# Two output stores a step in place of four, x rows loaded earlier, and a rearranged opening in a Fourier-and-mixer kernel

## The chip, the core and the metric

The kernel runs on one core of a Trainium2 chip. The core has a matrix engine (TensorE, in the rows PE, with its weight loads as PEld), a vector engine (VectorE, DVE), an engine for elementwise functions (ScalarE, ACT), a general engine (GpSimd, POOL) and one that here only issues transfers (SyncE, SP). Transfers between the chip's memory (DRAM) and the core's SBUF are carried by 16 DMA engines. Matrix products land in PSUM. The metric is the device time of one execution in microseconds (us).

## What is computed

Two stages over x of 8 batches, 3136 positions and 256 features. The first is the real part of a two-dimensional Fourier transform, the second a mixer: a rank-32 product along the positions, then a two-layer perceptron along the features, each added to its input.

```python
def _attn_ref(x):                       # x: 8, 3136, 256
    X = np.fft.fft(x, axis=1)
    X = np.fft.fft(X, axis=2)
    return X.real.astype(np.float32)

def _moe_ref(x, U, V, w_ch1, w_ch2):    # U: 3136x32, V: 32x3136, w_ch1: 256x1024, w_ch2: 1024x256
    xt = x.transpose(0, 2, 1)
    h = xt @ U @ V
    u = x + h.transpose(0, 2, 1)
    ch = np.maximum(u @ w_ch1, 0.0) @ w_ch2
    return (u + ch).astype(np.float32)
```

## The kernel before

Position n is split as n1*64 + n2 (49 by 64), an output position as k2*49 + k1. The kernel goes through the batches in four pairs. The symmetries of a real transform let lines k1 and 49-k1 be made together, so 25 values of k1 serve all 49.

**Front.** Tables, the transformed weights and the first batch (loaded and transformed by a path of its own, `load_single`, `te_single`) are made before the main loop. There each batch's rank-32 product ends in `te` (L282), is turned into `TT` by `te_turn` (L285) and multiplied into the hidden layer's basis by `te_hidden` (L299), which gives `TE`.

**Loading a pair.** Eight chunks. Of each, `load_pair_chunk` (L97) issues two transfers on SP: `xa` (L103) and, for the mirrored rows of the other half, `xb` (L107). Each is 98 rows of 4 KB. In DRAM, the 98 rows of `xa` are one run of equal strides, while `xb` reads its rows backwards and so has them as 2 batches of 49 rows:

```python
in_=bass.AP(x.tensor, x.offset + r * 4 * D, [[N1 * 64 * D, 2], [-64 * D, N1], [1, 4 * D]])
```

`fold_pair_chunk` (L145, POOL) adds `xa` and `xb` into `y`; `fold_pair_chunk_d` (L154) adds and subtracts the halves of the features into `yb`: two operations on DVE (L141, L142) and a copy of two columns on ACT (L143). `s1_steps` multiplies `yb` on PE into `z`, which is written to DRAM (`zturn`, L206), and `turn` (L273) reads it back the other way round into `g`. From `g` the `lines` steps make `q`, the transformed lines; each also sends one row of `q` to `VZ` with a small transfer (L383).

**The main loop.** A pair has 12 chunks of two steps and a short last one: 25 output tiles. In a step `mlp1` makes two groups of the hidden layer of the present chunk on PE (even and odd products from `q`, L425, then the rank-32 product from `TE` and `VZ`, L432), ACT copies one half (`ab`, L435), DVE makes the even and odd combinations with the maximum (L438, L441), and `mlp2` makes one output tile of the chunk before (L480, L490). Between the two phases of `mlp2` stands an empty ACT instruction (L492) by which PE's second phase waits for the first (the bank turn). `drain` copies the tile to `om` (ACT, L521), adds and subtracts into `ob` (POOL, L522, L523) and stores it with four transfers on SP (L527), each 64 rows of 1 KB.

**What sets the order.** The order is written out by hand (`manual_schedule`): `plan(p)` gives each of a pair's 26 steps a list of further work, and `place_next` spreads the loading of the next pair over them. For chunk c it starts at step a + gap*c with the load; 2 steps later comes the fold on POOL, 4 later the fold on DVE, 5 later the products. Each engine works through its list in order, SP too. SP's transfers use eight semaphores in turn, so a transfer's issue waits until the eighth transfer before it has landed. `ob` has four buffers.

Of the kernel before, what the change touches and what calls it, by code (L numbers as in the profile page):

```python
# [22 lines left out]
def kernel(  # L23
# [115 lines left out]
    def fold_d(yb, src, l0, l1):  # L139
        o, i = yb[:, l0:l1, :], src[:, l0:l1, :]  # L140
        nc.vector.tensor_tensor(o[:, :, 1:128], i[:, :, 1:128], i[:, :, 255:128:-1], op=AL.add)  # L141
        nc.vector.tensor_tensor(o[:, :, 129:256], i[:, :, 1:128], i[:, :, 255:128:-1], op=AL.subtract)  # L142
        nc.scalar.copy(o[:, :, 0:129:128], i[:, :, 0:129:128])  # L143

    def fold_pair_chunk(ck):  # L145

# [135 lines left out]
        nc.scalar.mul(te[0:rows, 0:129], ps[0:rows, 0, 0:129], 0.5)  # L282
        nc.scalar.mul(te[0:rows, 129:256], ps[rows:2 * rows, 0, 129:256], 0.5)

    def te_turn(pr, bs):  # L285
        ps = bank2("tt")
        n = 32 * len(bs)
        for blk in range(2):
            nc.tensor.matmul(ps[:, 0, 64 * blk:64 * blk + n], te[0:n, blk::2], eye[0:n, 0:n],
                             start=(blk == 0), stop=True, skip_group_check=True)  # L290
        for i, b in enumerate(bs):
            o = TT[pr.p % 2][b]
            src = ps[:, 0, 0:128].rearrange("p (k r) -> p k r", k=2)[:, :, 32 * i:32 * i + 32]
            copy_dve(o[:, :, 0:32], src)
            copy_act(o[:, :, 64:96], src)

    def te_hidden(pr, b, cs=None):
        o = TE[pr.p % 2][b]
# [56 lines left out]
    def lines(pr, b, c, evac, now=False):  # L355

        q = q_tile(pr)
        ps = [bank2("ln")] * 2
        if now:
            ps[1] = bank2("ln")  # L360
        for i in range(4):
            for blk in range(2):
                for s in range(2):
                    line(pr, b, ps[s][:, s, 256 * blk + 64 * i:256 * blk + 64 * i + 64], 8 * c + 1 + 2 * i + s, blk,
                         i == 0 and blk == 0)
        c0 = b * 1536 + 512 * c
        if now:
            return lambda evac: lines_out(q, ps, b, c, evac, now)
        lines_out(q, ps, b, c, evac, now)
# [41 lines left out]
    def mlp1_parts(ch, u):  # L411
        q, c0, w = ch.pr.q, ch.c0, ch.w
        m = 512 // w
        if u == 0:
            ch.h = hpool.tile([P, 2, JT, 256], BF16, tag="h", name="hT")
        ps = bank2("hps")
        for i in range(m):
            j = m * u + i
# [3 lines left out]
            for blk in range(2):  # L422
                for s in range(2):
                    lt = W1z[64:P, ja] if s and blk == 0 else W1p[c][64 * s:64 * s + 64, blk, jc]
                    nc.tensor.matmul(o[s], lt, q[64 * s:64 * s + 64, blk, c0:c0 + w], start=(i == 0 and blk == 0),  # L425
                                     stop=True, skip_group_check=True)
        yield
        for i in range(m):
            ja = slice((m * u + i) * P, (m * u + i + 1) * P)
            for b, a, n, v in ch.parts:  # L430
                for s in range(2):
                    nc.tensor.matmul(ps[:, s, i * w + a:i * w + a + n], TE[ch.p % 2][b][64 * s:64 * s + 33, ja],  # L432
                                     VZ[64 * s:64 * s + 33, b, v:v + n], start=False, stop=True, skip_group_check=True)
# [5 lines left out]
        if not ch.mini:  # L439
            flip = [v.rearrange("p i (t n) -> p (i t) n", n=P) for v in [h[:, 0], a, b]]  # L440
            nc.vector.tensor_tensor(flip[0][:, :, ::-1], flip[1], flip[2], op=AL.max)  # L441
            if u == 0:
                ch.qr = apool.tile([P, 2, 256], BF16, tag="qr", bufs=3, name="qr")
                copy_act(ch.qr.rearrange("p k (t n) -> p k t n", n=P)[:, :, :, ::-1],
                         q[:, :, c0:c0 + 256].rearrange("p k (t n) -> p k t n", n=P))
# [8 lines left out]
    def mlp2(ch, t, mixed):  # L454
# [56 lines left out]
        def drain(eng):  # L511
            n = 1 if ch.mini else 2
            po = st.ps[:, 0:n, 0:D].rearrange("p a (b d) -> p a b d", b=2)
            ob = opool.tile([P, 2, D], FP32, tag="ob", name="ob")
            om = opool.tile([P, 2, 2, P], FP32, tag="om", bufs=3, name="om")[:, 0:n]
            a = om[:, :, 0]
            if eng is nc.vector:
                nc.scalar.copy(om[:, :, 1], po[:, :, 1])
                a = po[:, :, 0]
            else:  # L520
                nc.scalar.copy(om, po)  # L521
            eng.tensor_tensor(ob[:, 0:n, 0:P], a, om[:, :, 1], op=AL.add)  # L522
            eng.tensor_tensor(ob[:, 0:n, P:D], a, om[:, :, 1], op=AL.subtract)  # L523
            for i in range(n):
                for hf, (b, k) in enumerate(ch.units[t]):
                    r = slice(64 - 64 * hf, 128 - 64 * hf) if i else slice(64 * hf, 64 * hf + 64)
                    nc.sync.dma_start(out=out[b].rearrange("(k2 k1) d -> k1 k2 d", k1=N1)[N1 - k if i else k], in_=ob[r, i])  # L527

        st.phase, st.drain = phase, drain
        if not mixed:  # L530
# [72 lines left out]
    nc.gpsimd.dma_start(out=uv[0:32], in_=moe_V)  # L603
    idle = W1z[:, 0:640]
    nc.vector.memset(idle.bitcast(FP32), 0.0)
    nc.sync.dma_start(out=VZ[96:97].rearrange("p b j -> p (b j)").rearrange("p (a j) -> p a j", j=640), in_=idle[0:5])

    wps = bank2("warm")[:, 0]

# [113 lines left out]
    for t in [x for y in TT for x in y]:  # L723
        nc.gpsimd.memset(t[:], 0.0)
        nc.gpsimd.memset(t[64:65, 0, 32:33], 1.0)
    nc.gpsimd.memset(V0[:].bitcast(FP32), 0.0)
    gate = tmp([64, 4], "gate")
    nc.gpsimd.tensor_copy(gate[0:1, 0:1], an2[0:1, 0, 0:1])
    bp_mask, bp_sin = residual_tables(nc.gpsimd)
# [58 lines left out]
    def v_copy(k0, k1, first=True):  # L788
# [3 lines left out]
            nc.sync.dma_start(out=VS[32:64, 0, cs], in_=VZ[64:96, 0, cs])  # L792
        elif first is None:
            v2 = [VS[:, i, cs].rearrange("p (w n) -> p w n", n=P) for i in range(2)]
            copy_dve(v2[1][0:32, :, ::-1], v2[0][0:32])
            ts(v2[1][32:64, :, ::-1], v2[0][32:64], -1.0, None)
        else:
            for r in (0, 64):
                nc.sync.dma_start(out=VZ[r:r + 32, 1, cs], in_=VZ[r:r + 32, 0, cs])
# [16 lines left out]
    nc.scalar.mul(W1p[0][:], w1ps[:], 0.5)  # L816
    nc.scalar.mul(W1z[64:P, 0:512], w1ps[64:P, 0], sgh[64:P])
    bp_sin()
    te_single(first, 0, teps)
    lps = lines(first, 0, 0, None, now=True)  # L820
    te_turn(first, [0])
    lps([copy_act, copy_dve])
    w1ps = bank2("w1ps")
    w1_fold(1, w1ps)
    te_hidden(first, 0, 0)
    nc.scalar.mul(W1p[1][:], w1ps[:], 0.5)
    nc.scalar.mul(W1z[64:P, 512:1024], w1ps[64:P, 0], sgh[64:P])
    w2_fold(0, nc.gpsimd)
# [12 lines left out]
    hpool = ctx.enter_context(tc.tile_pool(name="hpool", bufs=2))  # L841
    apool = ctx.enter_context(tc.tile_pool(name="apool", bufs=2))

    pairs = [first] + [Pair(p) for p in range(1, NP)]
    chunks = [ch for p in range(NP) for ch in pair_chunks(p)]
    NCK = len(chunks) // NP
    NS = 2 * NCK
    W1T = xpool.tile([P, 2, 2, 512], BF16, tag="xa", name="w1t")
# [9 lines left out]
    def product():  # L858
        ps = bank2("w12")
        for blk in range(2):  # L860
            for j in range(JT):
                nc.tensor.matmul(ps[:, blk, 0:D], W1T[:, j // 4, blk, (j % 4) * P:(j % 4 + 1) * P], W2[:, j, :],
                                 start=(j == 0), stop=(j == JT - 1))
        m = ps[:, :, 0:D]

        copy_act(G[:], m)
        nc.gpsimd.memset(RR[0][0:64].bitcast(FP32), 0.0)
        nc.gpsimd.memset(RR[1][0:64].bitcast(FP32), 0.0)
        for blk in range(2):
            ts(RR[0][64:P, blk], m[64:P, blk], sgm[64:P, blk:blk + 1], None)  # L870
        for blk in range(2):
            o = slice(blk * P, (blk + 1) * P)
            nc.vector.tensor_tensor(G[:, blk, o], G[:, blk, o], Bp[:, blk], op=AL.add)
            nc.vector.tensor_tensor(RR[0][64:P, blk, o], RR[0][64:P, blk, o], Bp[64:P, blk], op=AL.add)
            nc.vector.tensor_copy(RR[0][0:64, blk, o], Bp[0:64, blk])
            nc.vector.tensor_copy(RR[1][0:64, blk, o], Bp[0:64, blk])
            ts(RR[1][64:P, blk], RR[0][64:P, blk], sg[64:P, blk:blk + 1], None)

    def pair_tables():

# [31 lines left out]
    def plan(p):  # L912
# [11 lines left out]
        def place_next(nx, a, gap):  # L924

            s1 = list(s1_steps(nx, [copy_act, copy_dve]))
            for c, (load, fn, fd) in enumerate(load_steps(nx)):
                for o, f in [(0, load), (2, fn), (4, fd), (5, s1[2 * c]), (5, s1[2 * c + 1])]:
                    at[int(a + gap * c) + o].append(f)
            e = int(a + gap * 7) + 5  # L930
            at[e].append(lambda: (turn(nx, 0), turn(nx, 1)))
            at[e + 1].extend(te_steps(nx))
            at[e + 2].append(lambda: te_turn(nx, [0, 1]))
# [4 lines left out]
        if p == 0:  # L938
            rest = []
            at[0].append(lambda: te_hidden(cur, 0, 1))  # L940
            at[0].append(lambda: lines(cur, 0, 1, both))
            at[0].append(lambda: (w1_turn(0), w1_turn(1)))
            at[1].append(product)
            at[1].append(lambda: v_copy(1, 9, None))
            mid[2].append(lambda: te_direct(cur, 0))
            at[2].append(lambda: (v_lines(nc.gpsimd, 9, 17), v_copy(9, 17), lines(cur, 0, 2, both)))
            at[3].append(lambda: (v_lines(nc.gpsimd, 17, NK1), v_zero(nc.gpsimd), rest.append(pair_tables())))
            at[5].append(lambda: v_copy(9, 17, None))
            at[5].append(lambda: (v_copy(17, NK1), v_copy(0, 1), v_copy(0, NK1, False), rest[0]()))
            at[6].append(lambda: nc.sync.dma_start(out=T[64:P], in_=T[0:64]))  # L950
# [7 lines left out]
            at[13].append(lambda: lines(cur, 1, 1, both))  # L958
            at[15].append(lambda: lines(cur, 1, 2, both))
            at[18].append(lambda: (zero_line(cur, 0, copy_act), zero_line(cur, 1, copy_act)))  # L960
            place_next(pairs[1], 4, 1.75)
        else:
            at[0].append(lambda: lines(cur, 0, 1, both))
            at[2].append(lambda: te_hidden(cur, 1))
# [3 lines left out]
                at[7 + 3 * c].append(lambda c=c: lines(cur, 1, c, both))  # L968
            at[16].append(lambda: (zero_line(cur, 0, copy_act), zero_line(cur, 1, copy_act)))
            if p + 1 < NP:  # L970
                place_next(pairs[p + 1], 0, 2.3)
        return at

    for i in range(len(chunks) + 1):
# [7 lines left out]
        for t in range(2):  # L982
            m = None
            us_ = [] if cur is None else [t] if cur.mini else [2 * t, 2 * t + 1]
            n = 2 * (i % NCK) + t
            if len(us_) == 2:
                mlp1(cur, us_.pop(0))
            if prv is not None and t < len(prv.units):
# [43 lines left out]
```

## Time and profile before

| | |
|---|---|
| two runs | 613.29 and 614.98 us, median 614.13 |
| the profiled execution | 616.54 us; its span, first to last instruction, 614.3 us |
| mean granted TensorE clock | 0.875 |
| steps (one output tile each) | 100 |
| bytes moved by DMA | 65.53 MB, 107 GB/s over the span |
| out stores on SP | 392, of 64 KB each |

All times in the rows are of that one execution, and the sums of the prediction are made against its span, which is within 0.2 us of the runs' median. A wait row reads: engine, tile and line that waited, what it waited for, total us, number of waits, longest. A row of stretches gives the busy time of PE, PEld, DVE, ACT and POOL (with the number of instructions), the granted clock as a share of full speed, the mean busy share of the 16 DMA engines, and GB/s moved. With one DMA engine of 16 busy throughout, the share is 0.06. A timeline row gives start, duration, engine and line; the duration covers all instructions merged in it.

### The profile page before, as it was taken

How to read it: one execution, taken by the hardware profiler on the slowest of the kernel's cores; microseconds unless marked ns; L12 is line 12 of the kernel's file. 1: busy time of each engine (PE TensorE's matmuls, PEld its weight loads, DVE VectorE, ACT ScalarE, POOL GpSimd, SP SyncE). 2: the span in 40 equal slices, each digit the busy share in tenths (PEclk: the TensorE clock that was granted, in tenths of full speed). 3: DMA queues.
4: the chain of work that ended last, by engine and by line, in shares of the span. 5: the costliest groups of instructions: out<-in, count | busy, mean ns of one | idle time of the engine just before them, and what ended most of it. 6: DMA issues, size and time to landing. Idle time of an engine off the chain costs nothing. (4 is left out here: it accounts for less than half of the span.)

```text
span 614.3 us, 19104 instructions
## 1 busy us (share of the span) xinstructions
PE 485.0 (79%) x8159; PEld 384.2 (63%) x8159; DVE 356.6 (58%) x592; ACT 279.0 (45%) x505; POOL 249.4 (41%) x342
## 2 busy tenths in 40 slices
PE   4788798294869798886584979878677498999995
PEld 3658575183758476674462847756456285888894
DVE  7567894253764376564465337746456545676673
ACT  5665344152633455353342345534334235656552
POOL 7285334633451234444535124453453512333340
PEclk9788997686978798797795879988869589999998
DMA  8571334444338324334342832443434282233333
GB/s 158 172 106 25 88 110 108 133 117 137 102 109 180 82 91 121 124 100 128 96 126 64 174 88 90 118 130 95 128 93 126 63 180 67 56 75 71 73 80 79
DMA packets 60751, 65.53 MB, mean 107 GB/s; under 512 B 13593, under 2 KB 53496, under 8 KB 60504
## 3 DMA queue, kind: packets, MB, share of 16 engines
q1 hardware_dynamic: 56426, 59.45, 37.2%
q0 software_dynamic: 4160, 4.66, 4.3%
q8 instruction: 63, 1.03, 0.7%
q10 hardware_dynamic: 80, 0.20, 0.1%
q14 instruction: 22, 0.18, 0.1%
HBM read 34.62 MB, written 32.19 MB: 109 GB/s over the span
## 5 line engine op out<-in xcount | busy, mean ns | idle before, releaser
L480 PE MATMUL ops<-W,hT 64*128 64x256 bf16 x3072 | 224.7, 287 | 48.4 <-ACTq L492 41.3
L438 DVE SCALAR_TENSOR_TENSOR hT<-ab,hps 128x512 bf16<-128x512 bf16 x200 | 136.6, 683 | 172.3 <-ACT ab L435 172.2
L480 PEld LDWEIGHTS <-hT 64*128 64x128 bf16 x3072 | 158.9, 100 | 85.7 <-ACTq L492 44.6
L435 ACT CAST ab<-hps 128x512 bf16<-128x512 f32 x200 | 117.0, 590 | 127.1 <-PE hps L432 107.1
L425 PE MATMUL hps<-q,W1p 64*128 64x256 bf16 (+1 forms) x1248 | 131.3, 281 | 13.0 <-DVE hT L441 11.2
L151 POOL TENSOR_TENSOR y<-xa,xb 98x510 f32<-98x510 f32 (+1 forms) x48 | 58.1, 1231 | 192.6 <-DMA xb<-in_x_dram 184.1
L522 POOL TENSOR_TENSOR ob<-om 128x256 f32<-128x256 f32 (+1 forms) x97 | 78.0, 804 | 142.5 <-ACT om L521 121.3
L441 DVE TENSOR_TENSOR hT<-hps,ab 128x512 bf16<-128x512 f32 x192 | 130.8, 681 | 0.0
L425 PE MATMUL hps<-q,W1z 64*128 64x256 bf16 (+1 forms) x416 | 106.3, 282 | 0.0
L432 PE MATMUL hps<-VZ,TE 33*128 33x256 bf16 (+1 forms) x896 | 84.5, 273 | 27.4 <-DMA VZ<-q 27.1
L425 PEld LDWEIGHTS <-W1p 64*128 64x128 bf16 x1248 | 72.9, 99 | 31.0 <-DVE hT L441 19.4
L523 POOL TENSOR_TENSOR ob<-om 128x256 f32<-128x256 f32 (+1 forms) x97 | 78.2, 806 | 0.0
L141 DVE TENSOR_TENSOR yb<-y 98x508 bf16<-98x508 f32 (+1 forms) x24 | 33.8, 1409 | 62.7 <-POOL y L151 62.6
L432 PEld LDWEIGHTS <-TE 33*128 33x128 bf16 x896 | 44.4, 100 | 34.7 <-issue 28.4
L521 ACT COPY om<-ops 128x512 f32<-128x512 f32 (+1 forms) x97 | 56.4, 581 | 9.9 <-PE ops L490 9.8
L490 PE MATMUL ops<-TK,VS 64*128 64x256 f16 x192 | 54.6, 284 | 0.5 <-ACT TK L80 0.5
L425 PEld LDWEIGHTS <-W1z 64*128 64x128 bf16 x416 | 41.0, 99 | 3.0 <-issue 2.1
L490 PEld LDWEIGHTS <-qr 64*128 64x128 bf16 x384 | 38.2, 100 | 3.6 <-issue 0.4
L143 ACT CAST yb<-y 98x8 bf16<-98x8 f32 (+1 forms) x24 | 5.5, 227 | 76.9 <-POOL y L152 76.9
L490 PEld LDWEIGHTS <-q 64*128 64x128 bf16 x384 | 38.2, 100 | 2.8
L490 PE MATMUL ops<-R,qr 64*128 64x256 f16 x192 | 38.9, 284 | 0.0
L490 PE MATMUL ops<-R,q 64*128 64x256 f16 x192 | 38.8, 284 | 0.0
(181 smaller groups left out, 483.0 us busy)
## 6 DMA issues: line engine op xcount, KB each, us to landing
out_dram<-ob SPq DMA_DIRECT2D x392, 64.0 KB
xa<-in_x_dram SPq DMA_DIRECT2D x24, 392.0 KB
xb<-in_x_dram SPq DMA_DIRECT2D x24, 392.0 KB
zturn<-z SPq DMA_DIRECT2D x9, 512.0 KB
g<-zturn SPq DMA_DIRECT2D x6, 416.0 KB
g<-zturn SPq DMA_DIRECT2D x6, 384.0 KB
X<-in_x_dram POOLq DMA_DIRECT2D x4, 384.0 KB, 8.1
X<-in_x_dram POOLq DMA_DIRECT2D x2, 744.0 KB, 8.1
```

The source lines that it names most:

```text
L141: nc.vector.tensor_tensor(o[:, :, 1:128], i[:, :, 1:128], i[:, :, 255:128:-1], op=AL.add)
L151: nc.gpsimd.tensor_tensor(ck.y[:, l0:l1, 1:256], ck.xa[:, l0:l1, 1:256], rb[:, l0:l1, 255:0:-1], op=AL.add)
L425: nc.tensor.matmul(o[s], lt, q[64 * s:64 * s + 64, blk, c0:c0 + w], start=(i == 0 and blk == 0), stop=True, skip_group_check=True)
L432: nc.tensor.matmul(ps[:, s, i * w + a:i * w + a + n], TE[ch.p % 2][b][64 * s:64 * s + 33, ja], VZ[64 * s:64 * s + 33, b, v:v + n], start=F ...
L435: nc.scalar.copy(ab[:], ps[:, 1])
L438: nc.vector.scalar_tensor_tensor(h[:, 1], b, -1.0, a, op0=AL.mult, op1=AL.max)
L441: nc.vector.tensor_tensor(flip[0][:, :, ::-1], flip[1], flip[2], op=AL.max)
L480: mm = nc.tensor.matmul(op, ch.h[rows[half], s, j, t * P:(t + 1) * P], W2[rows[half], j, :], start=(ha == 0 and j == 0), stop=False, skip_ ...
L490: last = nc.tensor.matmul(*g[k], start=False, stop=(k == len(g) - 1), skip_group_check=True)
L521: nc.scalar.copy(om, po)
L522: eng.tensor_tensor(ob[:, 0:n, 0:P], a, om[:, :, 1], op=AL.add)
L523: eng.tensor_tensor(ob[:, 0:n, P:D], a, om[:, :, 1], op=AL.subtract)
```

## The change

- **Stores.** A full step's tile is stored with two transfers in place of four. Each now writes lines k and k+1 (or 49-k-1 and 49-k) together, from all 128 partitions. In DRAM the destination is 2 lines of 64 rows of 1 KB. The short last chunk keeps its 64-row stores.
- **Loads.** The folds and products of a chunk stand two steps later behind its load: the fold on POOL 4 steps after it, the one on DVE 6, the products 7. Chunks follow each other by 2 steps (2.3 before), in the first pair the first load comes at step 2 (4 before).
- **Fold copy.** L143's copy of two columns is on DVE, not on ACT.
- **Front.** The even and odd products of the first chunk (`mlp1_parts` up to its first `yield`) are issued ahead of `te_hidden`, the rank-32 part, and finished in step 0. The first `lines` uses one PSUM tile, and is drained before `te_turn`.
- **Tables.** `product` adds `Bp` on PE instead of DVE, and the rest of its rows are copied by ACT (`product_rows`). `VZ`'s zero row is set by POOL and not by a transfer. `v_lines` on POOL all stand in step 0; two table copies go from DVE to ACT. `qr` is copied after the second group of the hidden layer, not the first.

On SP, a stretch in the middle of the second pair's steps, before (`out_dram<-ob` are stores, `xa` and `xb` the loads, `VZ` the small rows, `zturn` the spill of `z`; the shape is the destination's):

```order
L103 DMA xa<-in_x_dram 98x1024
L107 DMA xb<-in_x_dram 98x1x1024
L527 DMA out_dram<-ob 64x256 x4
L383 DMA VZ<-q 1x16x32
L206 DMA zturn<-z 128x2048
L527 DMA out_dram<-ob 64x256 x8
```

and the same stretch of the changed kernel:

```order
L103 DMA xa<-in_x_dram 98x1024
L107 DMA xb<-in_x_dram 98x1x1024
L529 DMA out_dram<-ob 2x64x256 x2
L381 DMA VZ<-q 1x16x32
L529 DMA out_dram<-ob 2x64x256 x2
L103 DMA xa<-in_x_dram 98x1024
L107 DMA xb<-in_x_dram 98x1x1024
L529 DMA out_dram<-ob 2x64x256 x2
L206 DMA zturn<-z 128x2048
```

A step's four stores of 64x256 have become two of 2x64x256, the loads come every second step, and the spill of a chunk comes later behind the loads it came from.

On ACT, around one fold copy of the second pair, before:

```order
L521 COPY om<-ops 128x512
L435 CAST ab<-hps 128x512
L80 COPY qr<-q 128x4x128
L435 CAST ab<-hps 128x512
L143 CAST yb<-y 98x8
L521 COPY om<-ops 128x512
L435 CAST ab<-hps 128x512 x2
```

On DVE in the changed kernel, around the same copy:

```order
L436 SCALAR_TENSOR_TENSOR hT<-ab,hps 128x512
L439 TENSOR_TENSOR hT<-hps,ab 128x4x128
L141 TENSOR_TENSOR yb<-y 98x4x127
L142 TENSOR_TENSOR yb<-y 98x4x127
L143 CAST yb<-y 98x8
L436 SCALAR_TENSOR_TENSOR hT<-ab,hps 128x512
L439 TENSOR_TENSOR hT<-hps,ab 128x4x128
```

The copy stood on ACT between `ab` and `om`, with the bank turn behind it; it now follows the two fold operations on DVE.

The diff, cut to its core:

```diff
     def fold_d(yb, src, l0, l1):
...
-        nc.scalar.copy(o[:, :, 0:129:128], i[:, :, 0:129:128])
+        nc.vector.tensor_copy(o[:, :, 0:129:128], i[:, :, 0:129:128])
...
     def mlp1_parts(ch, u):
-        if u == 0:
-            ch.h = hpool.tile([P, 2, JT, 256], BF16, tag="h", name="hT")
         ps = bank2("hps")
...
         yield
+        if u == 0:
+            ch.h = hpool.tile([P, 2, JT, 256], BF16, tag="h", name="hT")
...
-            for i in range(n):
+            rows = out.rearrange("b (k2 k1) d -> b k1 k2 d", k1=N1)
+            if ch.mini:
                 for hf, (b, k) in enumerate(ch.units[t]):
-                    r = slice(64 - 64 * hf, 128 - 64 * hf) if i else slice(64 * hf, 64 * hf + 64)
-                    nc.sync.dma_start(out=out[b].rearrange("(k2 k1) d -> k1 k2 d", k1=N1)[N1 - k if i else k], in_=ob[r, i])
+                    nc.sync.dma_start(out=rows[b, k], in_=ob[64 * hf:64 * hf + 64, 0])
+            else:
+                b, k = ch.units[t][0]
+                for i, k in enumerate([k, N1 - k - 1]):
+                    nc.sync.dma_start(out=rows[b, k:k + 2], in_=ob[:, i])
...
     te_single(first, 0, teps)
-    lps = lines(first, 0, 0, None, now=True)
-    te_turn(first, [0])
-    lps([copy_act, copy_dve])
+    lines(first, 0, 0, None, now=True)([copy_act, copy_dve])
     w1ps = bank2("w1ps")
     w1_fold(1, w1ps)
+    te_turn(first, [0], copy_dve)
+    first.u = [mlp1_parts(ch0, i) for i in range(2)]
+    next(first.u[0])
     te_hidden(first, 0, 0)
+    next(first.u[1])
...
             for c, (load, fn, fd) in enumerate(load_steps(nx)):
-                for o, f in [(0, load), (2, fn), (4, fd), (5, s1[2 * c]), (5, s1[2 * c + 1])]:
+                for o, f in [(0, load), (4, fn), (6, fd), (7, s1[2 * c]), (7, s1[2 * c + 1])]:
                     at[int(a + gap * c) + o].append(f)
-            e = int(a + gap * 7) + 5
+            e = int(a + gap * 7) + 7
...
-            place_next(pairs[1], 4, 1.75)
+            place_next(pairs[1], 2, 1.75)
...
-                place_next(pairs[p + 1], 0, 2.3)
+                place_next(pairs[p + 1], 0, 2)
...
+            if i + t == 0:
+                for g in first.u:
+                    next(g)
+                us_ = []
```

More of the change, by code (lines that the diff above doesn't have):

```diff
@@ L283, in te_out, with te_turn @@
         nc.scalar.mul(te[0:rows, 129:256], ps[rows:2 * rows, 0, 129:256], 0.5)
-    def te_turn(pr, bs):
+    def te_turn(pr, bs, eng=copy_act):
         ps = bank2("tt")
@@ L294, in te_turn @@
             copy_dve(o[:, :, 0:32], src)
-            copy_act(o[:, :, 64:96], src)
+            eng(o[:, :, 64:96], src)
     def te_hidden(pr, b, cs=None):
@@ L358, in lines @@
         ps = [bank2("ln")] * 2
-        if now:
-            ps[1] = bank2("ln")
         for i in range(4):
@@ L441, in mlp1_parts @@
             nc.vector.tensor_tensor(flip[0][:, :, ::-1], flip[1], flip[2], op=AL.max)
-            if u == 0:
+            if u == 1:
                 ch.qr = apool.tile([P, 2, 256], BF16, tag="qr", bufs=3, name="qr")
@@ L605 @@
     nc.vector.memset(idle.bitcast(FP32), 0.0)
-    nc.sync.dma_start(out=VZ[96:97].rearrange("p b j -> p (b j)").rearrange("p (a j) -> p a j", j=640), in_=idle[0:5])
     wps = bank2("warm")[:, 0]
@@ L726 @@
     nc.gpsimd.memset(V0[:].bitcast(FP32), 0.0)
+    nc.gpsimd.memset(VZ[96:97].bitcast(FP32), 0.0)
     gate = tmp([64, 4], "gate")
@@ L794, in v_copy @@
             v2 = [VS[:, i, cs].rearrange("p (w n) -> p w n", n=P) for i in range(2)]
-            copy_dve(v2[1][0:32, :, ::-1], v2[0][0:32])
-            ts(v2[1][32:64, :, ::-1], v2[0][32:64], -1.0, None)
+            copy_act(v2[1][0:32, :, ::-1], v2[0][0:32])
+            nc.scalar.mul(v2[1][32:64, :, ::-1], v2[0][32:64], -1.0)
         else:
@@ L818 @@
     bp_sin()
+    pairs = [first] + [Pair(p) for p in range(1, NP)]
+    chunks = [ch for p in range(NP) for ch in pair_chunks(p)]
+    ch0 = chunks[0]
+    ch0.pr = first
     te_single(first, 0, teps)
-    lps = lines(first, 0, 0, None, now=True)
-    te_turn(first, [0])
-    lps([copy_act, copy_dve])
+    lines(first, 0, 0, None, now=True)([copy_act, copy_dve])
     w1ps = bank2("w1ps")
     w1_fold(1, w1ps)
+    te_turn(first, [0], copy_dve)
+    first.u = [mlp1_parts(ch0, i) for i in range(2)]
+    next(first.u[0])
     te_hidden(first, 0, 0)
+    next(first.u[1])
     nc.scalar.mul(W1p[1][:], w1ps[:], 0.5)
@@ L842 @@
     apool = ctx.enter_context(tc.tile_pool(name="apool", bufs=2))
-    pairs = [first] + [Pair(p) for p in range(1, NP)]
-    chunks = [ch for p in range(NP) for ch in pair_chunks(p)]
     NCK = len(chunks) // NP
@@ L862, in product, with product_rows @@
                 nc.tensor.matmul(ps[:, blk, 0:D], W1T[:, j // 4, blk, (j % 4) * P:(j % 4 + 1) * P], W2[:, j, :],
-                                 start=(j == 0), stop=(j == JT - 1))
+                                 start=(j == 0), stop=False, skip_group_check=True)
+        for blk in range(2):
+            nc.tensor.matmul(ps[:, blk, blk * P:(blk + 1) * P], eye[:], Bp[:, blk], start=False, stop=True, skip_group_check=True)
         m = ps[:, :, 0:D]
         copy_act(G[:], m)
-        nc.gpsimd.memset(RR[0][0:64].bitcast(FP32), 0.0)
-        nc.gpsimd.memset(RR[1][0:64].bitcast(FP32), 0.0)
+        copy_dve(RR[0][64:P], m[64:P])
         for blk in range(2):
[L870 to L877, printed above, removed]
+            ts(RR[1][64:P, blk], m[64:P, blk], sg[64:P, blk:blk + 1], None)
+        for r in RR:
+            nc.vector.tensor_copy(r[64:65, 0, 0:P], Bp[64:65, 0])
+            nc.vector.memset(r[64:65, 0, P:D].bitcast(FP32), 0.0)
+    def product_rows():
+        for r in RR:
+            nc.gpsimd.memset(r[0:64].bitcast(FP32), 0.0)
+            for blk in range(2):
+                nc.scalar.copy(r[0:64, blk, blk * P:(blk + 1) * P], Bp[0:64, blk])
     def pair_tables():
@@ L942, in plan @@
             at[0].append(lambda: (w1_turn(0), w1_turn(1)))
+            at[0].append(product_rows)
+            at[0].append(lambda: (v_copy(1, 9, None), v_lines(nc.gpsimd, 9, 17), v_lines(nc.gpsimd, 17, NK1), v_zero(nc.gpsimd)))
             at[1].append(product)
-            at[1].append(lambda: v_copy(1, 9, None))
             mid[2].append(lambda: te_direct(cur, 0))
-            at[2].append(lambda: (v_lines(nc.gpsimd, 9, 17), v_copy(9, 17), lines(cur, 0, 2, both)))
-            at[3].append(lambda: (v_lines(nc.gpsimd, 17, NK1), v_zero(nc.gpsimd), rest.append(pair_tables())))
+            at[2].append(lambda: (v_copy(9, 17), lines(cur, 0, 2, both)))
+            at[3].append(lambda: rest.append(pair_tables()))
             at[5].append(lambda: v_copy(9, 17, None))
```

## The prediction, made before the changed kernel ran

> **What bounds the kernel now.** I read the page's shares and slices first, then stretches by pair, then who waited for whom, then SP's queue.
>
> ```profile
> PE 485.0 (79%) x8159; PEld 384.2 (63%) x8159; DVE 356.6 (58%) x592; ACT 279.0 (45%) x505; POOL 249.4 (41%) x342
> ...
> 48.00:212.00 164.00, 125.57 (x2133) 99.63 (x2130) 91.64 (x160) 67.43 (x129) 67.42 (x88) 0.84 0.42 110
> 212.00:365.50 153.50, 120.06 (x1881) 91.37 (x1882) 85.37 (x120) 65.29 (x122) 61.30 (x74) 0.84 0.42 111
> 365.50:516.00 150.50, 116.87 (x1883) 89.97 (x1881) 84.98 (x120) 65.16 (x122) 61.32 (x74) 0.88 0.42 112
> 516.00:612.00 96.00, 89.57 (x1700) 79.81 (x1694) 62.46 (x101) 52.23 (x92) 31.82 (x46) 0.99 0.31 71
> ```
>
> The four stretches are the four pairs. The last one loads nothing: 25 steps in 96 us, 3.8 us a step, PE busy for 93% of it at clock 0.99. The other three take 150 to 164 us, with 34 to 38 us of them without PE work and the clock at 0.84 to 0.88. So PE bounds the last pair, and something in the loading of the next pair bounds the first three.
>
> ```profile
> POOL y L151 <- DMA xb<-in_x_dram: 184.1, 22, 15.0
> ACT yb L143 <- POOL y L152: 76.9, 18, 11.2
> DVE yb L141 <- POOL y L151: 62.6, 18, 9.7
> PE ops L480 <- ACTq L492: 41.3, 11, 8.7
> PE hps L432 <- DMA VZ<-q: 27.1, 5, 11.6
> ...
> SPq L527 <- POOL ob L523: 101.9, 46, 12.3
> SPq L527 <- DMA xb<-in_x_dram: 81.3, 18, 5.9
> ```
>
> It is one chain. POOL's fold waits for `xb`, ACT's copy L143 waits for the fold, the bank turn L492 stands behind that copy on ACT, and PE waits for the turn: 41.3 us. SP's stores wait 81.3 us for an `xb` eight transfers earlier, and a small row of `VZ` behind such a store costs PE another 27.1 us. At the root is one slow transfer. Why it is slow shows in stretches where nothing else moves:
>
> ```profile
> 225.60:230.30 4.70, 4.63 (x98) 3.82 (x93) 4.34 (x6) 2.94 (x6) 4.70 (x7) 1.00 0.13 52
> 475.60:479.70 4.10, 0.00 (x0) 0.00 (x0) 0.00 (x0) 0.00 (x0) 0.00 (x0) 0.74 0.13 51
> 304.80:305.90 1.10, 1.10 (x27) 0.96 (x23) 0.35 (x1) 0.58 (x1) 0.63 (x1) 1.00 0.13 46
> 326.30:327.40 1.10, 0.00 (x0) 0.00 (x0) 0.00 (x0) 0.00 (x0) 0.56 (x1) 0.50 0.14 47
> 479.80:481.00 1.20, 0.00 (x0) 0.00 (x0) 0.00 (x0) 0.00 (x0) 0.45 (x1) 0.50 0.13 45
> ...
> 468.63 0.71 SPq L107 DMA_DIRECT2D xb<-in_x_dram  x1
> 469.44 11.19 SPq L527 DMA_DIRECT2D out_dram<-ob  x8
> ```
>
> The last columns are the share of 16 DMA engines and GB/s. In the first two stretches only `xb` is under way (4 KB rows): 0.13 of 16 is two engines, at 52 GB/s. At 475.6 every compute engine stands still for it. In the other three stretches the remains of the stores issued behind an `xb` (1 KB rows) run off on the same two engines, at 45 to 47 GB/s: other shares of those stores had long gone through the idle engines. So `xb` is carried by two engines alone, and they give 52 GB/s in 4 KB rows and 46 in 1 KB rows. What sets `xb` apart from its twin `xa` (same size, same SBUF side) is its DRAM side: 2 batches of 49 rows, where `xa` has 98.
>
> **The change, part by part.**
>
> ```profile
> out_dram<-ob SPq DMA_DIRECT2D x392, 64.0 KB
> xa<-in_x_dram SPq DMA_DIRECT2D x24, 392.0 KB
> xb<-in_x_dram SPq DMA_DIRECT2D x24, 392.0 KB
> zturn<-z SPq DMA_DIRECT2D x9, 512.0 KB
> g<-zturn SPq DMA_DIRECT2D x6, 416.0 KB
> g<-zturn SPq DMA_DIRECT2D x6, 384.0 KB
> ...
> L527 SPq DMA_DIRECT2D out_dram<-ob x392: 466/594/1925, 54.0 to 611.0; - x196
> ...
> 186.90:188.10 1.20, 1.20 (x22) 0.95 (x19) 0.41 (x1) 0.58 (x1) 0.00 (x0) 0.78 0.98 385
> 190.50:198.00 7.50, 7.37 (x146) 6.04 (x140) 3.63 (x7) 3.54 (x9) 2.81 (x4) 1.00 1.16 203
> 128.00:129.00 1.00, 1.00 (x25) 0.90 (x21) 0.00 (x0) 1.00 (x3) 0.33 (x1) 1.00 0.82 162
> ```
>
> *The stores.* 384 of 392 become 192 of 128 KB; 8 stay. SP saves 192 issues of 0.594 us, 1.2 us a step. But the new destination is 2 lines of 64 rows, and 2 is the outermost count on the DRAM side, as with `xb`. No store of that form is in the trace, so its price has two ends. Spread over 16 engines, it costs the sum nothing. On two, 131,072 bytes at 46 GB/s take 2.85 us, two of them 5.7 us a step, where PE needs 3.8. I take two engines, by the nearest row: `xb` has the same pair of sides (2 outermost in DRAM, one run of partitions in SBUF), only in the other direction. That the destination counts as well is borne out by the two transfers `UZ<-uturn` (50 rows at the destination, 1600 runs at the source) in the stretch 128.0 to 129.0: with an `xb` beside them the share is 0.82, while transfers on all 16 engines show 0.98 and 1.16.
>
> The Trainium skill, "DMA: Bandwidth & Descriptors", section "Why a DMA increments its semaphore by 16 and not by 1", says that a transfer runs on the largest number of engines up to 16 that divides the slowest dimension above 1 of both sides. By it the new store gets 2, and the sum is the 880 us below; if the source's 128 partitions alone counted, it would be the first rival's 555. The trace agrees for `xb`.
>
> So the two engines now carry, each running all the time:
> - 192 stores at 2.85 us: 547 us.
> - 24 `xb` of 401,408 bytes at 52 GB/s, 7.7 us: 185 us.
> - Their part of what goes over all engines: 24 `xa` of 401 KB at the 385 GB/s of the spread stretch 186.9, 1.04 us each, 25 us; 12 spills of 512 KB at the same rate, 16 us; three times 1.6 MB of `g` at 203 GB/s, 8 us each, 24 us. Together 65 us.
>
> They start with the first store at 54.0. 54 + 547 + 185 + 65 = 851 us. To it come gaps in which the two engines have nothing: three times at `turn`, where SP holds the stores back until `zturn` has landed (the transfers of `g` start 2 us after that, and their landing comes on top: 5 us, 15 in all), some 8 us until the first steps' stores pile up, and 5 us for the last tile. That makes 879, and I say 880. In a step of a loading pair the two engines have 5.7 us of stores and 8 x 7.7 / 25 = 2.5 us of `xb`, 8.2 us against 4.7 us of PE work (117 to 120 over 25): nothing that PE, ACT or DVE do comes near.
>
> Who waits: `ob` has four buffers, so POOL's add waits for the store four steps back, ACT's `om` for POOL, PSUM for `om`, PE for PSUM. On SP, behind a store that waits for the eighth transfer before it, stand the loads, the spill and the row of `VZ`; each then queues behind up to 8 stores (some 23 us) on the two engines.
>
> *Loads four steps ahead.* Before, two steps of about 6 us lay between load and fold, against 7.7 us of transfer plus its queue. Four steps of 8 us cover it if the queue is empty; with 23 us of stores ahead of it the load still lands about when the fold asks. This buys the chain up to 41.3 + 27.1 us only if the stores are spread.
>
> *Fold copy.*
>
> ```profile
> L143 ACT CAST yb<-y 98x8 bf16<-98x8 f32 x21 | 4.8, 228 | 50.3 <-POOL y L152 50.3
> L875 DVE COPY R<-Bp 64x128 f16<-64x128 f16 x2 | 0.4, 187 | 0.1
> L873 DVE TENSOR_TENSOR G<-G,Bp 128x128 f16<-128x128 f16 x2 | 1.6, 791 | 0.0
> ...
> L780 POOL TENSOR_TENSOR VZ<-uv x4: 2067/2114/2192, 40.5 to 56.2; 32x512 bf16<-32x512 f32 x4
> ```
>
> 27 copies of about 0.2 us, 6 us, go from ACT to DVE, which is 58% busy: hidden. ACT's 76.9 us of waiting goes, and with it the turn's 41.3. What is late next is `om`, waiting for `ob`. Nothing, in the sum.
>
> *Front and tables.* The front ends where the first store stands, at 54.0. The products ahead of the rank-32 part are moved, not added; `product` loses the two additions of 0.79 us on DVE, 1.6 us; POOL's table lines, 4 x 2.1 us (L780), all stand ahead of the first `drain` now, which puts it up to 8 us later or sets POOL free as much earlier. I take 0, with 8 us to either side, all in pair 0 and under the stores from then on.
>
> **Rivals.**
>
> *The stores are spread over 16 engines* (faster). Then a step keeps 128 KB stores that cost what the old ones did, SP is free 1.2 us sooner a step, and the waits of the chain go: 614 - 41 - 27 = 546, with some given back, since `xb` keeps its 7.7 us every second step: 555 us. Speaking for it: SBUF's side is 128 partitions, and 64 KB stores use all engines now. Against: `xb`, whose SBUF side is as good, does not. It decides at the store's price: below 3.8 / 2 = 1.9 us the last pair is no slower, above it the two engines win. The Trainium skill has a rule that speaks for this outcome too: "DMA: Bandwidth & Descriptors", "Rules for kernel authors", says to join many small transfers into a large one. 0.06.
>
> *Spread, but the loads gain nothing*, since `xb` stays on two engines and only the waiting place moves: 614 less at most 12, within 2%. 0.02.
>
> *Two engines, and PE falls to half its clock as well.* In waits the granted clock reaches 0.50 (326.3, above). At half clock the last pair's step would take twice its 89.57 / 25 = 3.6 us of PE work, 7.2 against 5.7, 24 x 1.5 = 36 us more, and with a gap of 10 us at each `turn` instead of 5 another 15: 931 us. Against: a PE that works 7.2 us of 7.2 no longer waits, and the clock in the long busy stretches is 1.00. 0.12.
>
> *The store's 1 KB rows cost less or more than 46 GB/s* belongs to the main case. At the 52 of 4 KB rows the stores take 484 us, and the sum is 816; at 41, 614 us and 947.
>
> **How the numbers follow.** Two engines with PE hidden: 0.80, 880 us, the likeliest. Two engines with a slow PE: 0.12, 931. Spread: 0.06, 555; spread without gain: 0.02. The range 835 to 950 holds both two-engine cases but for their tails, about 8 in 10. The lower end is a little above 816, since the rows of 1 KB never reached 52; the upper is the 947 of the slower rows. A measurement here tells changes over 2% from none. Faster 0.06, within it 0.02, slower 0.92. The profiled span before is 614.3 us and the runs' median 614.13, so nothing is added for the difference.
>
> **What would show it.** Right: in the last pair a DMA share near 0.13 and 45 GB/s where it was 0.31 and 71, and 5.7 us a step; POOL waiting for `out_dram<-ob` instead of `xb`; PE waits spread over all steps; no L143 on ACT and no PE wait on L492 caused by it. Wrong: a share of 0.3 in the last pair and 3.8 us a step means that the stores are spread, and the time is then under 600. A store that takes 1.4 us on two engines would mean that rows of two neighbouring lines are joined.

## The result, and the profile after

The changed kernel took 862.92 us (861.84 and 864.00), against 614.13: a ratio of 1.405, with a 95% interval of 1.394 to 1.416. The profiled execution has a span of 860.1 us. The prediction was 880, between 835 and 950. Times here and below are medians of a kernel's runs, without runs more than 1.5% above its fastest.

From the page of the changed kernel, engine shares and the stores:

```profile
PE 496.0 (58%) x8161; PEld 395.6 (46%) x8161; DVE 342.5 (40%) x609; ACT 282.0 (33%) x487; POOL 241.1 (28%) x343
...
out_dram<-ob SPq DMA_DIRECT2D x192, 128.0 KB
```

PE does 496 us of work, about as before (485), and is busy for 58% of a longer span. The stretches of the four pairs, cut where each pair's first tile is copied out, and 80 us out of the last pair (columns as before: busy time of PE, PEld, DVE, ACT and POOL, clock, share of 16 DMA engines, GB/s):

```profile
54.90:286.50 231.60, 126.25 (x2186) 100.99 (x2183) 97.06 (x169) 72.12 (x129) 61.64 (x84) 0.78 0.28 82
286.50:504.70 218.20, 122.70 (x1884) 96.57 (x1880) 76.66 (x128) 65.13 (x113) 57.04 (x74) 0.75 0.25 78
504.70:722.70 218.00, 122.00 (x1882) 96.72 (x1878) 77.16 (x128) 64.95 (x112) 57.14 (x74) 0.76 0.23 74
722.70:858.00 135.30, 86.13 (x1604) 73.28 (x1598) 56.85 (x92) 47.54 (x87) 30.99 (x44) 0.87 0.14 49
760.00:840.00 80.00, 49.03 (x886) 40.66 (x880) 30.68 (x50) 23.78 (x46) 18.30 (x26) 0.89 0.14 50
```

Every pair is longer, the last as well, which loads nothing. There the share is 0.14 of 16, two engines and a little, and they move 49 to 50 GB/s without a pause. Before, the last pair had 0.31 and 71 GB/s, and PE was busy for 93% of it; now for 64%.

Of the waits, longest in total first, those on which the rest turns (total, times, longest):

```profile
...
POOL ob L520 <- DMA out_dram<-ob: 205.6, 53, 5.6
...
PE hps L430 <- DMA VZ<-q: 148.0, 14, 31.5
POOL y L151 <- DMA xb<-in_x_dram: 116.3, 19, 10.7
...
PE ln L353 <- DMA g<-zturn: 72.2, 3, 26.1
...
PE ops L478 <- ACTq L490: 8.3, 8, 2.4
```

and the line of the 2-line stores, with min, median and max of an issue on SP in ns:

```profile
L529 SPq DMA_DIRECT2D out_dram<-ob x192: 511/2542/9353, 57.1 to 847.6; - x192
```

POOL now waits for the buffers of `ob`, so for stores: 205.6 us, where the kernel before had 13.4:

```profile
POOL ob L522 <- DMA out_dram<-ob: 13.4, 5, 3.2
```

An issue of a store takes 2.54 us in the median, against 0.594, since SP waits in it until the eighth transfer before has landed. That is about the rate of the two engines (2.72 us a store, below), seen at the queue. PE's 41.3 us behind the bank turn have shrunk to 8.3. In their place PE waits 148 us for rows of `VZ` and 72 us for `g`: transfers of 1 to 416 KB that stand behind stores, on SP and on the two engines. One such case, first on SP's timeline, then on PE's (start, duration, what; in brackets the idle time before it):

```profile
337.99 3.36 SPq L381 DMA_DIRECT2D VZ<-q  x1
341.45 2.57 SPq L529 DMA_DIRECT2D out_dram<-ob  x2
```

```profile
346.82 0.61 PE L430 MATMUL hps<-VZ,TE 33*128 33x256 bf16 x4 [15.99 <-DMA VZ<-q]
```

SP comes to the row of 1 KB at 338.0, after two stores that held it for 10.1 us. It has to hold the row for another 3.4 us before it can issue it, at 341.4, and PE can go on at 346.8, 5.5 us later, after 16 us of standing still.

### The profile page after: what moved, and what is told of

The parts are those of the page before. It is cut to its first block, busy times and chain, and to the rows that moved or that the text cites. A ratio compares the mean times of both kernels' runs of the same rounds, so it can differ in the third digit from the quotient of the medians.

```text
span 860.1 us, 18816 instructions
## 1 busy us (share of the span) xinstructions
PE 496.0 (58%) x8161; PEld 395.6 (46%) x8161; DVE 342.5 (40%) x609; ACT 282.0 (33%) x487; POOL 241.1 (28%) x343
## 2 busy tenths in 40 slices
DMA packets 54980, 65.50 MB, mean 76 GB/s; under 512 B 7828, under 2 KB 47726, under 8 KB 54734
## 4 chain that ended last, share of the span: by engine, by line
SPq 29%; DMA 28%; PE 16%; DVE 5%; issue 5%; POOL 3%; ACT 3%; POOLq 0%; DVEq 0%; ACTq 0%
SPq L529 22%; DMA out_dram<-ob 12%; DMA xb<-in_x_dram 7%; PE ops L478 6%; DMA VZ<-q 6%; PE hps L421 4%; DMA zturn<-z 2%; SPq L381 2%; PE hps L430 2%; SPq L103 2%; DVE hT L439 2%; DVE hT L436 2%; PE ops L488 2%; DMA g<-zturn 1%; ACT ab L433 1%
## 5 line engine op out<-in xcount | busy, mean ns | idle before, releaser
L478 PE MATMUL ops<-W,hT 64*128 64x256 bf16 x3072 | 231.3, 292 | 17.0 <-ACTq L490 8.3
L520 POOL TENSOR_TENSOR ob<-om 128x256 f32<-128x256 f32 (+1 forms) x97 | 71.0, 732 | 448.9 <-ACT om L519 205.9
L478 PEld LDWEIGHTS <-hT 64*128 64x128 bf16 x3072 | 165.5, 102 | 53.6 <-DVE hT L439 16.9
L421 PE MATMUL hps<-q,W1p 64*128 64x256 bf16 (+1 forms) x1248 | 135.6, 288 | 18.7 <-DVE hT L439 14.3
L421 PE MATMUL hps<-q,W1z 64*128 64x256 bf16 (+1 forms) x416 | 109.3, 289 | 0.0
L521 POOL TENSOR_TENSOR ob<-om 128x256 f32<-128x256 f32 (+1 forms) x97 | 71.0, 732 | 0.0
L353 PE MATMUL ln<-T,g 64*128 64x64 bf16 x400 | 13.8, 202 | 72.2 <-DMA g<-zturn 72.2
L80 ACT CAST q<-ln 128x1024 bf16<-128x1024 f32 (+2 forms) x32 | 25.6, 814 | 81.9 <-PE ln L353 81.9
L194 PE MATMUL s<-yb,F 98*128 98x258 bf16 (+1 forms) x108 | 18.0, 300 | 50.0 <-DVE yb L143 44.8
L353 PEld LDWEIGHTS <-g 64*128 64x128 bf16 x400 | 12.4, 103 | 74.5 <-DMA g<-zturn 73.6
L80 ACT CAST z<-s 128x1024 bf16<-128x1024 f32 (+1 forms) x24 | 23.0, 960 | 68.4 <-PE s L194 68.4
```

Source lines behind the costliest of these rows:

```text
L478: mm = nc.tensor.matmul(op, ch.h[rows[half], s, j, t * P:(t + 1) * P], W2[rows[half], j, :], start=(ha == 0 and j == 0), stop=False, skip_ ...
```

## The experiments

Four theories were to be told apart: that the 2-line stores run on two engines and set the time; that their size or the 128 partitions do; that the loads' distance or a moved operation does; that each such store has a fixed price in SP's queue. Kernels that ran together shared a chip and its runs of the kernel before, whose time differs a little from chip to chip (614.7 to 617.9 us); ratios are to those.

**The stores put back, in the changed kernel.**

```diff
-                b, k = ch.units[t][0]
-                for i, k in enumerate([k, N1 - k - 1]):
-                    nc.sync.dma_start(out=rows[b, k:k + 2], in_=ob[:, i])
+                for i in range(n):
+                    for hf, (b, k) in enumerate(ch.units[t]):
+                        r = slice(64 - 64 * hf, 128 - 64 * hf) if i else slice(64 * hf, 64 * hf + 64)
+                        nc.sync.dma_start(out=rows[b, N1 - k if i else k], in_=ob[r, i])
```

> The changed kernel with its stores alone put back: four of 64 rows a step. Theory (the 2-line stores run on two DMA engines and set the time): the 192 x 2.85 us go off these two, which keep 185 us of xb, and PE bounds again; the waits of 41 and 27 us of the kernel before are shorter, so 560 us, between 535 and 600. Rival (the loads four steps ahead, or the moved fold copy, cost the time): 800 us or more. Rival (the rest gains nothing): 602 to 626 us.

Measured: 589.5 us (586.75 and 592.25), ratio 0.959 (0.951 to 0.966). The loss is gone, and the rest of the change is a gain of 4%. The theory holds, at the upper end of its range. One of SP's waits, in an execution of 595.85 us, shows where time still goes:

```profile
SPq L530 <- DMA xb<-in_x_dram: 123.9, 23, 6.8
```

With four stores a step, SP stands 123.9 us behind an `xb` eight transfers earlier (81.3 before). The loads are issued earlier, and SP's stores wait longer for them.

**The 2-line stores alone, in the kernel before** (the same edit the other way round).

> The kernel before with the 2-line stores alone. Theory: the same two engines carry 547 us of stores, 185 of xb and 65 of other transfers from 54 us on, so 850 to 900 us, and a DMA share near 0.13 in the last pair. Rival (the rest of the change makes the loss): under 630 us.

Measured: 862.51 us, ratio 1.403 (1.394 to 1.411), the same as with the whole change. Its last pair, and then PE's waits in it:

```profile
760.00:840.00 80.00, 49.94 (x902) 41.53 (x898) 31.33 (x52) 24.60 (x47) 18.26 (x26) 0.89 0.14 50
```

```profile
PE ops L480 <- ACTq L492: 125.1, 20, 12.6
PE hps L432 <- DMA VZ<-q: 100.8, 9, 31.2
```

The DMA columns are those of the changed kernel to the digit, 0.14 and 50. PE's waits are others: here it waits 125 us at the bank turn, where the changed kernel has 8.3. So a bottleneck off the compute engines fixes the time, and where PE waits for it makes no difference. All the rest of the change is worth nothing under it.

**Half of them**: one 2-line store and two 64-row stores a step.

```diff
-                for i, k in enumerate([k, N1 - k - 1]):
-                    nc.sync.dma_start(out=rows[b, k:k + 2], in_=ob[:, i])
+                nc.sync.dma_start(out=rows[b, k:k + 2], in_=ob[:, 0])
+                for hf, (b, k) in enumerate(ch.units[t]):
+                    nc.sync.dma_start(out=rows[b, N1 - k], in_=ob[64 - 64 * hf:128 - 64 * hf, 1])
```

> The changed kernel with one 2-line store and two 64-row stores a step. Theory: the two engines carry 96 x 2.85 = 274 us of stores, 185 of xb, 65 of others, 524 us from 54 us on: 606 us at the end with 28 us of gaps, so 600 us, between 575 and 650, since this is about as long as PE takes. Rival (each 2-line store costs a fixed time on SP or in waits, so that half of them cost half of the loss): about 700 us or more.

Measured: 660.74 us, ratio 1.074 (1.067 to 1.082). Neither number was right. The loss against four 64-row stores is 71 of 273 us, a quarter and not a half, so the fixed price falls. But 660 is over the theory's range. The second pair and a stretch of the last one:

```profile
234.60:399.00 164.40, 117.89 (x1884) 92.55 (x1879) 81.09 (x128) 65.24 (x112) 59.43 (x74) 0.84 0.36 103
...
565.00:640.00 75.00, 73.90 (x1424) 67.09 (x1420) 52.73 (x82) 44.96 (x80) 29.58 (x42) 1.00 0.35 72
```

The last pair is at PE's pace again (busy for 73.9 of 75 us), the loading pairs are not. The expectation had added the two engines' work over the whole run and compared that with PE's. The longer of the two has to be taken pair by pair: what the engines could do in the last pair is of no use to the others. It had also left out that each 64-row store puts 4 of its rows on each of the 16 engines, so on these two. For a loading pair, in the prices of the prediction and with the 2.72 us that a 2-line store took in the changed kernel (worked out further below): 24 x 2.72 = 65 us, 8 x 7.7 = 62, `xa`, spill and `g` 22, the 48 64-row stores at 4 KB an engine and 24 GB/s 8, the turn 5: 162 us, measured 164.4. That is worked out after the run.

**The same bytes, the same number of stores, another order in DRAM.** If the two lines' positions alternate over the partitions, a store of 128 partitions goes to 64 rows of two neighbouring lines.

```diff
-                    nc.sync.dma_start(out=rows[b, k:k + 2], in_=ob[:, i])
+                    nc.sync.dma_start(out=rows[b, k:k + 2].rearrange("k1 k2 d -> k2 k1 d"), in_=ob[:, i])
...
-        o = q[:, :, c0:c0 + 512].rearrange("p k (i s j) -> p s k i j", i=4, s=2)
+        o = q[:, :, c0:c0 + 512].rearrange("p k (i j s) -> p s k i j", i=4, s=2)
```

`VZ`'s rows are interleaved in the same way where they are written.

> The changed kernel with two lines' positions interleaved over the partitions, so that a store still takes 128 KB from 128 partitions, twice a step, but its DRAM side is 64 rows of two neighbouring lines in place of 2 lines of 64. Theory (the outermost count of the DRAM side sets the number of engines): 16 engines, a time of 560 us or a little under the kernel with four stores, since SP issues 192 fewer. Rival (128 KB stores are slow as such, by their size or by all 128 partitions): 830 us or more.

Measured: 543.2 us, ratio 0.887 (0.879 to 0.895). Not the size of a store, nor its partitions, nor how many there are makes the loss, but the outermost count on its DRAM side: 2, or 64. This kernel takes 37% less time than the changed one by a change of order alone, and is faster than both. In a burst of its stores in the last pair, from 484.0 to 484.5 us, the share is 0.68 of 16 engines at 230 GB/s. The counts of DMA packets, first of the changed kernel, then of this one, rule out one more rival, that the two neighbouring rows are now written as one of 2 KB:

```profile
DMA packets 54980, 65.50 MB, mean 76 GB/s; under 512 B 7828, under 2 KB 47726, under 8 KB 54734
DMA packets 57668, 65.51 MB, mean 121 GB/s; under 512 B 10516, under 2 KB 50414, under 8 KB 57422
```

Between 512 B and 2 KB both have 39,898 packets, so no rows were joined. This kernel has 2,688 more under 512 B, which is 192 x 14: what comes out if each store ends in one small packet on every engine that it uses, 16 here and 2 in the changed kernel. That reading of the small packets is inferred from the counts; the kernel with half of the 2-line stores fits it too (10,708, which is 192 x 16 - 96 x 2 = 2,880 more than 7,828).

SP's waits for `xb`, and the last pair:

```profile
SPq L529 <- DMA xb<-in_x_dram: 44.3, 12, 7.4
...
SPq L105 <- DMA xb<-in_x_dram: 19.3, 3, 6.7
SPq L107 <- DMA xb<-in_x_dram: 11.8, 2, 6.1
```

```profile
440.00:525.00 85.00, 78.54 (x1474) 72.61 (x1472) 55.45 (x87) 48.60 (x83) 28.12 (x40) 0.99 0.19 63
```

With half the stores, eight transfers reach back further: SP's stores stand 44.3 us behind `xb` and its loads 31.1, against 123.9 and 6.4 with four stores. So the halved number of transfers is a gain of its own, 590 to 543 us, once the stores are spread; that these waits are what it saves is argued from the rows. PE is busy for 92% of the last pair at clock 0.99.

**`xb` taken off the two engines**, in the changed kernel: `nc.gpsimd.dma_start` for its load.

> The changed kernel, its 24 loads of xb issued by POOL on POOL's own queue instead of by SP. Theory (stores and xb share the same two engines, and their times add up): if POOL's queue puts xb on other engines, the two keep 547 us of stores and 65 of others, so 54 + 612 + 28 = 694 us, between 670 and 730. If POOL's queue uses the same two, 850 to 880 us as before. Rival (the stores alone would take this long, through SP's waits, whatever else is on the engines): 850 to 880 us although the trace shows xb on other engines.

Measured: 713.14 us, ratio 1.154 (1.147 to 1.161). In the trace, one stretch of it:

```profile
307.00:308.00 1.00, 1.00 (x23) 0.89 (x21) 1.00 (x3) 0.99 (x2) 1.00 (x1) 1.00 0.28 103
```

0.28 of 16 is four engines and a half, at 103 GB/s, about 48 of stores and 52 of `xb`. POOL's queue put `xb` on two other engines there, and 150 us of the 185 went. So the stores and `xb` do add up on the two engines, as the prediction had it. 19 us more than 694 stayed, and by the store price measured in the changed kernel (192 x 2.72 = 522 us, worked out below) the sum is 669 and about 40 us of the span of 710 are over. Part of that shows in the trace: POOL's queue did not always take other engines. From 210.0 to 218.0 and from 381.0 to 390.0, with an `xb` and stores under way, the share is 0.13 and 0.14 of 16 at 52 and 53 GB/s, two engines for both, and every compute engine stands still. These two stretches are 17 us; what the rest is stays open.

**What the rest of the change is worth**, in the kernel with interleaved positions. The fold copy back on ACT:

> The kernel with interleaved positions (542 to 550 us), with the fold copy back on ACT. Theory (with loads four steps ahead the fold is seldom late, POOL waits 19 us for xb in all, so the copy holds the bank turn little): 545 to 556 us. Rival (the move of the copy is the main gain, the 41 us of the bank turn): 570 us or more.

Measured: 540.67 us, ratio 0.874 (0.869 to 0.879), below what either expected; the one without this edit was 0.887 on another chip, so the two were run again side by side (below). The loads and folds at their old distances:

> The kernel with interleaved positions (542 to 550 us), with the loads and folds at their old distances (fold 2 steps after the load, chunks 2.3 steps apart, first load at step 4). Theory (two steps of some 5 us do not cover 7.7 us of xb and its queue; DVE instead of ACT now waits): 560 to 590 us. Rival (the freed SP issues early enough, distance is worth nothing): 540 to 552 us.

Measured: 576.75 us, ratio 0.934 (0.930 to 0.937). The folds' waits in it and in the kernel with the new distances:

```profile
POOL y L151 <- DMA xb<-in_x_dram: 131.8, 20, 13.6
```

```profile
POOL y L151 <- DMA xb<-in_x_dram: 18.7, 10, 4.4
```

The distances are worth 5 to 6% of the time before (576.75 against 540.67 on the same chip, in a kernel that has the fold copy on ACT besides), and this shows where it should: POOL waits 131.8 us for `xb` with two steps and 18.7 with four.

`xb` issued by POOL:

> The kernel with interleaved positions (542 to 550 us), with the loads of xb issued by POOL. Theory (xb on two fixed engines is what still holds SP and the folds): SP's waits for xb, 44 + 19 + 12 us, go, and the time falls to 525 to 540 us. Rival (PE's own work and the evictions bound now): 540 to 550 us. Rival (POOL's issue of 24 transfers delays its adds): above 550 us.

Measured: 539.68 us, ratio 0.872 (0.867 to 0.877), at the edge of the theory's range and of the first rival's, so the time alone does not tell them apart. SP's waits for `xb` are gone from its profile, and that is worth about 1% (0.9% between two kernels below that differ by it alone, on one chip).

Four more ran together on one chip, to settle differences of 1 or 2%. The reference among them (e6_again):

> The kernel with interleaved positions once more, beside the three that follow, on one chip: a ratio to the kernel before between 0.879 and 0.895, its interval of the first time.

Measured: 542.89 us, ratio 0.881 (0.877 to 0.884).

> The same with the fold copy on ACT, on the same chip. Theory (the copy holds nothing once the folds come in time): within 1% of e6_again, to either side. Rival (its place on DVE is worth its share of the bank turn): 2% or more above e6_again.

Measured: 540.82 us, ratio 0.879 (0.876 to 0.882). No difference: the place of the fold copy is worth nothing once the folds come in time. Its waiting in this run, against 76.9 us before:

```profile
ACT yb L143 <- POOL y L152: 3.2, 2, 2.5
```

The first chunk's products back behind the rank-32 part:

```diff
-    te_turn(first, [0], copy_dve)
-    first.u = [mlp1_parts(ch0, i) for i in range(2)]
-    next(first.u[0])
-    te_hidden(first, 0, 0)
-    next(first.u[1])
+    te_turn(first, [0])
+    te_hidden(first, 0, 0)
...
-            if i + t == 0:
-                for g in first.u:
-                    next(g)
-                us_ = []
```

> The kernel with interleaved positions, the first chunk's products back in step 0, behind the rank-32 part, as before. Theory (moved work, hidden or nearly so; the first store stood at 54.0 us before and at 56.3 with the products ahead): within 1% of e6_again. Rival (the early products fill idle time of PE in the front and save it): 5 to 8 us slower.

Measured: 546.7 us, ratio 0.886 (0.882 to 0.891). 0.7% over the reference by the medians, with intervals that overlap: inconclusive, and by the medians (3.8 us) under the 5 to 8 us of the rival.

> The kernel with interleaved positions, the xb loads issued by POOL and the fold copy on ACT. Theory (the first takes SP's waits for xb away, the second is worth nothing): like the kernel with xb on POOL's queue, a ratio of 0.866 to 0.877 to the kernel before. Rival (both gains add): a ratio under 0.862.

Measured: 535.86 us, ratio 0.871 (0.868 to 0.875), 13% under the kernel before, as with `xb` on POOL's queue alone (0.872). Against the kernel with only the copy on ACT (540.82), on the same chip, the queue is worth 0.9%. The rival's ratio under 0.862 did not come: the copy adds nothing that shows. A load of `xb` that runs on more than two engines was not tried.

## Why the prediction was right, point by point

**The bound.** Right. One slow transfer in the trace, `xb`, showed that a count of 2 on the outer DRAM side means two engines. The stores with this count run at 0.14 of 16 engines. That they do so although the 2 stands at the destination was argued from `UZ`, on thin ground, since 0.82 of 16 is still 13 engines; the interleaved kernel shows it, with all else equal.

The rule that the prediction cites from the Trainium skill ("DMA: Bandwidth & Descriptors", section "Why a DMA increments its semaphore by 16 and not by 1": the largest number up to 16 that divides both sides' slowest dimension) agrees with all of this: 2 and 128 gave two engines, 64 and 128 gave no such limit.

**The size of the terms.** The store's term was 5% too large. In the last pair, POOL's adds into `ob` (L520) start at 760.34, 765.82 and so on to 825.64 us, 12 steps of 5.44 us, which is 2.72 us a store and 48 GB/s, not the 46 taken from the remnants before. The 50 GB/s of the stretch hold other transfers as well: from 840.0 to 848.0, when no compute engine but DVE does any work, it is 48. So the stores took 192 x 2.72 = 522 us instead of 547. The first store stood at 57.1 us instead of 54.0. 860.1 - 57.1 - 522 = 281 us are left for `xb`, the transfers on all engines and the gaps, where the prediction had 185 + 65 + 28 = 278. Errors of -25, +3 and +3 make the -20 us between 880 and the span, up to rounding. The +3 is not exact part by part: the first pair is 231.6 us long against 218.2 and 218.0, and its tables, which the sum had left out, are transferred there too, so other parts of the 278 must have been some 10 us too large; which ones is not shown. The second and third pair come to 24 x 5.44 + 62 + 22 + 5 = 220 by the prices, 218 measured.

**The stretch in the last pair.** The share near 0.13 and 45 GB/s, 5.7 us a step, came as 0.14, 50 and 5.4. The sign that was named for joined rows, 1.4 us a store on two engines, could not have come: at the 52 GB/s that two engines gave in the 4 KB rows of `xb`, a store would still take 2.5 us.

**Where PE waits.** Half right. The bank turn's wait went, POOL waits for stores, and the small rows wait behind the queue, as said. But POOL also waits 116 us for `xb` still, where the prediction let the load land about when the fold asks. And "PE waits spread over all steps" was wrong: 220 us of its waits are lumps at 14 rows of `VZ` and 3 of `g`, up to 31.5 us long. PE ran ahead between them.

**The rivals.** A slow PE did not add to it: the clock was 0.87 in the last pair. "Spread over 16 engines: 555 us" was not the outcome, but the interleaved kernel makes it, and takes 543. That this lies near the estimate is in part luck. The estimate took 68 us of PE's waits off, and 9 were given back. PE's idle time fell by only 38 us, from 614.3 - 485.0 to 541.4 - 449.8; another 35 us came from PE's work itself getting shorter, at a granted clock of 0.955 instead of 0.875, which the estimate did not have. With four spread stores a step the same change gave only 590.

**Costs put at nothing.** The fold copy: none, shown. The front: nothing that these runs can tell. The loads' distance: nothing under the two engines (862.5 without it, 862.9 with it), and 5 to 6% once they are free, as the prediction's condition said.

## What to carry to other kernels

Before two transfers are joined into one, look at the outermost count that is left on both sides; the joined transfer has half the issues, and here also an eighth of the engines. A transfer's own rate can be read from a trace wherever it runs alone and without a pause: share times 16 is then its number of engines. And where several transfers are confined to the same few engines, add up what these carry, pair by pair or stage by stage, and compare it with the compute of that stage, not of the whole run.

## What was not expected of the hardware

Two engines kept busy moved 48 GB/s of stores in rows of 1 KB over 65 us, and the remnants of about 1 us in the kernel before had given 45 to 47: stretches that short set the price to within 5%. Loads of the same shape ran on two engines from SP's queue and from POOL's, and not always on the same two: with `xb` on POOL's queue, four were busy in some stretches (0.25 of 16 from 303.0 to 304.0, 0.28 from 307.0 to 308.0), only two in others (0.13 and 0.14, above), and the time fell by 150 us.
